# Cosine attention and a two-layer MLP in one kernel: three value and weight loads of GpSimd in another order

## The chip, the cores and the metric

One core of a Trainium2 chip. The metric is the device time of one execution in microseconds (us). The kernel before takes 432.26 us, the median of 3 runs (431.92 to 432.89).

## The reference

Eight batches, 12 heads, 448 positions, head size 64. Attention first, with queries and keys scaled to unit length:

```
q_n = q / (norm(q) + 1e-6);  k_n = k / (norm(k) + 1e-6)
scores = q_n @ k_n^T / tau
attn   = exp(scores - max) / (sum + 1e-9)
x      = (attn @ v), heads side by side          # 3584 x 768
h      = x @ w_in                                # 768 x 2048
out    = max(0.01 h, h) @ w_out                  # 2048 x 768
```

All inputs are float32, and so is the output.

## The kernel before

**Units of work.** A *pair* is two heads of one batch: 6 pairs to a batch, 48 in all, numbered by `s`. A *quad* is two pairs: 3 to a batch, 24 in all, numbered by `j`. The 448 positions of a sequence are 384 in three tiles of 128, and 64 left over; the leftovers of two pairs are packed together ("rem"). A *chunk* `c` is the 384 or 512 rows of the MLP that follow a batch.

**A pair's path.** `load_qk` (SP's queue) loads q and k in float32; the load pool has four buffers, so pair s+4 takes the place of pair s. `squares` (GpSimd) and `sums` (VectorE) give the sums of squares, `roots` (ScalarE) the norms, `normalise` (VectorE) the scaled bf16 tile `qn`. `transposes` turns it into `qkT` (TensorE up to pair 11, then by DMA). `scores` and `key_tiles` multiply on TensorE (L253), and ScalarE takes the exponential (L265). Ahead of each pair's squares `hold` has GpSimd cast one column of `qn` into a small tile, `seen`: it makes GpSimd wait there until VectorE has normalised a certain pair.

**A quad's path.** `attend(j)` runs `totals(j)` (products of the exponentials with ones, L276; then the reciprocal on ScalarE by Ln and Exp), two strips of `products(j, e)` with the values, also L276, and `scale(j, e)` on VectorE into `xT`. The products need two things from the values: `v_b`, the 384 main positions of that quad (`load_v(j)`, 192 KB, L143), and `v_rem`, the left-over 64 positions of a whole batch (`load_v_rem(b)`, four loads of 24 KB, L151; two tiles, by even and odd batch). In a strip the products with `v_b` come first (12 matmuls), then those with `v_rem` (4).

**The MLP.** `first(c, m)` is one of 16 groups of the first layer (L330), with a leaky ReLU on ScalarE (L337). `second(c, ts, half)` is 16 matmuls of the second layer (L360) for one half of the output's columns, which read that half of `w_out_sb`. For chunk 0 all of half 0 comes before half 1. The weights come by GpSimd's queue, cast from float32 to bf16: `load_w_in` in four parts of 768 KB (L106), `load_w_out(half)` in two of 1536 KB (L112).

**Order.** The schedule is written by hand; each engine runs its instructions in program order. First a loop over the six pairs of batch 0 (L468 to L523); its last slot, s == 5, is the one that is changed. Then a stretch written out (L536 to L574): `attend(2)`, and the preparation of pairs 7 to 10 between 13 of the 16 groups of chunk 0's first layer, with `load_v(4)` and `load_w_out(1)` in it. Then a planner's loop over batches 1 to 7: in each unit it places `attend`, three score tiles, the preparation of a pair ahead, and as many MLP groups as its share says. Its first unit for batch 1 begins with `attend(3)` and `load_v(5)`.

In the sixth slot GpSimd does, in order: `hold`, `squares(8)`, `load_w_out(0)`, `load_v(3)`, `load_v_rem(1)`. Quad 3 is the first of batch 1; `load_v(3)` and `load_v_rem(1)` are the values that `attend(3)` reads.

Of the kernel before, what the change touches and what calls it, by code (L numbers as in the profile page):

```python
# [16 lines left out]
def kernel(  # L17
# [59 lines left out]
    def banks(count, keep=None, which=None):  # L77
        lo, hi = (0, 8) if not deals["apart"] else (0, 4) if count == 2 else (4, 8)
        x = which if which is not None else min(
            (i for i in range(lo, hi, count) if not set(range(i, i + count)) & set(kept.values())),  # L80
            key=lambda i: max(age[i : i + count]),
        )
        deals["n"] += 1
        age[x : x + count] = [deals["n"]] * count
        if keep:
            kept[keep] = x
        return ps[:, x] if count == 1 else ps[:, x : x + count]
# [16 lines left out]
    def load_w_in(i):  # L104
        n0, e = i // 2 * (D_ff // 2), i % 2
        gp.dma_start(  # L106
            out=w_in_sb[:, e::2, n0 : n0 + D_ff // 2], in_=w_in_r[e, :, :, n0 : n0 + D_ff // 2]
        )

    def load_w_out(half):  # L110
        n0 = half * HALF
        gp.dma_start(out=w_out_sb[:, :, n0 : n0 + HALF], in_=w_out_r[:, :, n0 : n0 + HALF])  # L112
# [6 lines left out]
    def load_qk(s, engs=(nc.sync, nc.sync)):  # L119
        if s >= NSLOT:  # L120
            return
        b, h0 = s // NPAIR, 2 * (s % NPAIR)
        q_h = ldp.tile([128, 2, 4, D], F32, name="q_h")
        k_h = ldp.tile([128, 2, 3, D], F32, name="k_h")
        engs[0].dma_start(out=q_h[:, :, 0:3], in_=main(q, b, h0, 2))  # L125
        engs[1].dma_start(out=k_h, in_=main(k, b, h0, 2))
        for i, (x, eng) in enumerate(zip((q, k), engs)):
            eng.dma_start(  # L128
                out=q_h[64 * i : 64 * i + 64, :, 3],
                in_=x[b, h0 : h0 + 2, MAIN:S].rearrange("h p d -> p h d"),  # L130
            )
        raw[s] = (q_h, k_h)
# [5 lines left out]
    def load_v(j):  # L138
        if j >= B * NQ:
            return  # L140
        b, jj = divmod(j, NQ)
        vb[j] = vbp.tile([128, 4, 3, D], BF16, name="v_b")
        gp.dma_start(out=vb[j], in_=main(v, b, 4 * jj, 4))  # L143

    def load_v_rem(b):
        if b >= B:
            return
        r = v[b, :, MAIN:S].rearrange("(j g) p d -> g p j d", g=4)
        for g in range(4):
            lo = 64 * (g // 2)  # L150
            gp.dma_start(out=vrb[b % 2][lo : lo + 64, :, g], in_=r[g])  # L151
# [3 lines left out]
    def squares(s, engs=(gp, gp)):  # L155
        if s >= NSLOT:
            return
        tiles = []
        for x, eng, name in zip(raw[s], engs, ("sq0", "sq1")):
            sq = sqp.tile(list(x.shape), F32, name=name)  # L160
            if eng is nc.scalar:
                nc.scalar.activation(sq, x, func=AF.Square)
            else:
                eng.tensor_tensor(sq, x, x, op=ALU.mult)  # L164
            tiles.append(sq)
        sqs[s] = tiles

    def sums(s, parts=(0, 1)):
        if s >= NSLOT:
            return  # L170
        if s not in ss:
            ss[s] = smp.tile([128, 14], F32, name="ss")
        for i in parts:
            o = ss[s][:, 0:8] if i == 0 else ss[s][:, 8:14]
            nc.vector.tensor_reduce(  # L175
                o.rearrange("p (h t) -> p h t", h=2), sqs[s][i], axis=AX.X, op=ALU.add
            )

    def roots(s):
        if s >= NSLOT:  # L180
            return
        nc.scalar.activation(ss[s], ss[s], func=AF.Ln, bias=tiny)
        nc.scalar.activation(ss[s], ss[s], func=AF.Exp, scale=0.5)
        nc.scalar.activation(ss[s], ss[s], func=AF.Identity, bias=eps)  # L184
# [3 lines left out]
    def normalise(s):  # L188
        if s >= NSLOT:
            return  # L190
        r = smp.tile([128, 14], F32, name="r")
        nc.vector.reciprocal(r, ss[s])  # L192
        qn[s] = qnp.tile([128, 7, 2, D], BF16, name="qn")
        for x, lo, hi, r0 in ((raw[s][0], 0, 4, 0), (raw[s][1], 4, 7, 8)):
            nt = hi - lo
            nc.vector.tensor_tensor(  # L196
                qn[s][:, lo:hi],
                x.rearrange("p h t d -> p t h d"),
                r[:, r0 : r0 + 2 * nt].rearrange("p (h t) -> p t h", h=2)
                .unsqueeze(3).to_broadcast([128, nt, 2, D]),  # L200
                op=ALU.mult,
            )
# [19 lines left out]
    def transposes(s):  # L222
        if s >= NSLOT:
            return
        dst = qtp.tile([128, 7, 128], BF16, name="qkT")
        qkT[s] = dst.rearrange("p t c -> p (t c)")
        if s >= DMA_FROM:
            nc.sync.dma_start(
                out=dst, in_=qn[s].rearrange("p t h d -> p (t h d)"), transpose=True
            )  # L230
            return
        tp = transposed()
        one(tp, s, 0, 7)
        nc.vector.tensor_copy(out=dst, in_=tp)
# [3 lines left out]
    def scores(s, kis):  # L238
        key_tiles([(s, ki) for ki in kis])
# [53 lines left out]
    def products(j, e, po=None):  # L293
        b, jj = divmod(j, NQ)
        if po is None:
            po = banks(1, (j, e))
        pos[j, e] = po
        vm = vb[j].rearrange("p h t (d e) -> p h t e d", e=2)
        vr = vrb[b % 2].rearrange("p j g (d e) -> p j g e d", e=2)
        strip_products(j, po, lambda g, ki: vm[:, g, ki, e], lambda g: vr[:, jj, g, e])  # L300

    def scale(j, e):
        b, jj = divmod(j, NQ)
        m, half = divmod(b, 2)
        if m not in xT:
            xT[m] = xtp.tile([128, KT, 2 * S], BF16, name="xT")
        nc.vector.tensor_tensor(  # L307
            xT[m][:, 2 * jj + e, half * S : (half + 1) * S], pos.pop((j, e))[:, :S], rbs[j],
            op=ALU.mult,
        )  # L310
        if (j, e) in kept:
            given_back((j, e))
# [115 lines left out]
    def fill(count):  # L428
        wm = banks(1)
        for i in range(count):  # L430
            nc.tensor.matmul(
                out=wm, lhsT=warm[:, :128], rhs=warm, start=(i == 0), stop=(i == count - 1)
            )
# [4 lines left out]
    def hold(x):  # L438
        seen = smp.tile([128, 1], F32, name="seen")
        gp.tensor_copy(out=seen, in_=x)  # L440
# [27 lines left out]
    for s in range(NPAIR):  # L468
        j = s // 2 - 1 if s >= 2 else None
        even = s % 2 == 0  # L470
        n = s + 2 if s + 2 <= NPAIR else None
        if s != 3 and s != 5:
            scores(s, (0,))
        if s == 1:
            roots(2)
        if j is not None and not even:
            products(j, 1)
        scores(s, (1,))
        fill(2)
        if s and n:  # L480
            sums(n, (0,))
        normalise(s + 1)
        load_qk(s + 5)
        if j is not None and not even:
            scale(j, 0)
        hold(qn[s + 1][:, 6, 0, 0:1])
        squares(s + 3)
        if s == 5:
            load_w_out(0)
        if not even:  # L490
            load_v(s // 2 + 1)
        if s != 2 and s < 5:
            load_w_in(s - s // 3)
        if s == 5:
            load_v_rem(1)
        if n:
            sums(n, (1,))
        scores(s, (2,))
        if s == 5:

            scale(j, 1)
            for m in range(SOON):
                pms[0, m] = banks(1, (0, m, 0), 4 + m)
            first(0, 0, range(KT - 2))
        elif not even:
            fill(2)
        if not even:
            scores(s, (3,))
        transposes(s + 1)
        if s == 0:  # L510
            sums(2, (0,))
        if s == 5:
            first(0, 1, range(KT - 2))
        elif not even:
            fill(2)
        if n and s:
            roots(n)
        if j is not None and not even and s < 5:
            scale(j, 1)
        if j is not None and even:  # L520
            totals(j)
            scores(s + 1, (0,))
            products(j, 0)  # L523
# [11 lines left out]
    s, j = NPAIR, NQ - 1  # L535
# [61 lines left out]
    for b in range(1, B):  # L597
# [3 lines left out]
        for i, (at, tiles, ahead) in enumerate(units):  # L601
# [8 lines left out]
            s = b * NPAIR + ahead if ahead else NSLOT  # L610
# [63 lines left out]
```

## Time and profile before

| What | Value |
|---|---|
| Median of 3 runs | 432.26 us |
| Profiled execution, first to last instruction | 433.2 us |
| TensorE busy | 418.9 us, 97% |
| ScalarE busy | 267.7 us, 62% |
| VectorE busy | 188.4 us, 43% |
| GpSimd busy | 138.1 us, 32% |
| Mean granted TensorE clock | 0.995 |
| GpSimd's transfer queue | 25056 packets, 11.80 MB |
| SP's transfer queue | 77296 packets, 40.98 MB |

The profile is of a single execution; 433.2 us is its span, and of its own time no other figure is given. It is 0.96 us above the median of the timed runs. In the rows below, PE is TensorE, PEld its weight loads, DVE VectorE, ACT ScalarE, POOL GpSimd and SP SyncE; Lnnn is a line of the kernel before. "[1.18 <-DMA v_b...]" means that the engine sat idle for 1.18 us before the row and that a landing of `v_b` ended it.

### The profile page before, as it was taken

Reading aid. Unit: us, or ns where it says so; the run is one execution under the profiler, and the core shown is the slowest. Engines: PE = TensorE matmul, PEld = TensorE weight load, DVE = VectorE, ACT = ScalarE, POOL = GpSimd, SP = SyncE. Lnnn points to the kernel's source line nnn. Section 1 sums busy time; section 2 is a strip of 40 time slices with the busy share of each in tenths; the row PEclk is TensorE's granted clock in tenths of the full one; section 3 lists DMA queues with packets and bytes.
Section 4 is the critical chain, followed back from the end, with each engine's and each line's share of the span. In section 5 each row is a group of like instructions: output and inputs, shape, how many; then the busy total and the mean of one; then the engine's idle time right before and its main releaser. Section 6 shows DMA issues by size and latency. Waiting matters only on the chain.

```text
span 433.2 us, 8650 instructions
## 1 busy us (share of the span) xinstructions
PE 418.9 (97%) x3329; PEld 209.0 (48%) x3329; DVE 188.4 (43%) x366; ACT 267.7 (62%) x494; POOL 138.1 (32%) x208
## 2 busy tenths in 40 slices
PE   8699989999999999999999999999999999999995
PEld 3234535544455555544455555554455555554563
DVE  5875846643353544552444544643434432220021
ACT  4997846668654787658745687668845496434300
POOL 4767523261424133531334114432234120000000
PEclk9999989999999999999999999999999999999999
DMA  7999994795548447765448557666437532010022
GB/s 173 196 236 232 219 212 65 166 189 142 105 106 164 100 126 142 162 109 142 86 105 159 102 144 146 140 113 160 82 86 162 101 80 41 36 74 2 0 74 73
DMA packets 102889, 53.65 MB, mean 124 GB/s; under 512 B 68929, under 2 KB 97857, under 8 KB 102849
## 3 DMA queue, kind: packets, MB, share of 16 engines
q1 hardware_dynamic: 77296, 40.98, 37.9%
q0 software_dynamic: 25056, 11.80, 21.6%
q8 instruction: 26, 0.43, 0.4%
q10 hardware_dynamic: 496, 0.33, 0.2%
q14 instruction: 15, 0.11, 0.1%
HBM read 45.61 MB, written 11.01 MB: 131 GB/s over the span
## 4 chain that ended last, share of the span: by engine, by line
PE 85%; DMA 8%; POOL 3%; SPq 1%; DVE 1%; ACT 0%; issue 0%; POOLq 0%; DVEq 0%
PE ps L360 34%; PE ps L330 31%; PE ps L276 12%; PE ps L253 8%; DMA v_rem<-in_v_dram 5%; DMA q_h<-in_k_dram 3%; POOL sq L164 1%; DMA q_h<-in_q_dram 1%; SPq L128 1%; DVE qn L196 1%; POOL v_b L143 0%; POOL v_rem L151 0%; POOL w_out_sb L112 0%; PE ps L210 0%; SPq L125 0%
## 5 line engine op out<-in xcount | busy, mean ns | idle before, releaser
L265 ACT ACTIVATE pe<-ps 128x896 bf16<-128x896 f32 x144 | 122.5, 917 | 53.0 <-PE ps L253 52.0
L330 PE MATMUL ps<-xT,w_in_sb 128*128 128x384 bf16 (+1 forms) x768 | 151.4, 353 | 0.7 <-DVE xT L307 0.7
L360 PE MATMUL ps<-w_out_sb,hT 128*128 128x384 bf16 x896 | 151.9, 326 | 0.0
L360 PEld LDWEIGHTS <-hT 128*128 128x128 bf16 x896 | 85.2, 98 | 62.9 <-issue 8.0
L330 PEld LDWEIGHTS <-w_in_sb 128*128 128x128 bf16 x768 | 73.1, 98 | 73.1 <-issue 8.1
L337 ACT ACTIVATE hT<-ps 128x384 bf16<-128x384 f32 (+1 forms) x128 | 65.1, 540 | 40.1 <-PE ps L330 39.5
L440 POOL CAST seen<-qn 128x1 f32<-128x1 bf16 x47 | 8.7, 185 | 210.4 <-DVE qn L196 210.4
L371 DVE COPY osb<-ps 128x384 f32<-128x384 f32 (+1 forms) x56 | 30.9, 552 | 97.3 <-PE ps L360 90.9
L175 DVE TENSOR_REDUCE ss<-sq 128x8 f32<-128x512 f32 (+1 forms) x96 | 56.8, 613 | 18.5 <-POOL sq L164 16.5
L253 PE MATMUL ps<-qkT 64*128 64x448 bf16 (+1 forms) x384 | 46.7, 362 | 4.2 <-ACT pe L265 2.9
L164 POOL TENSOR_TENSOR sq<-q_h 128x512 f32<-128x512 f32 x46 | 47.8, 1039 | 5.0 <-DMA q_h<-in_k_dram 4.2
L192 DVE RECIPROCAL r<-ss 128x14 f32<-128x14 f32 x48 | 11.6, 241 | 82.3 <-ACT ss L184 82.3
L307 DVE TENSOR_TENSOR xT<-ps,rb 128x448 bf16<-128x448 f32 x48 | 27.9, 619 | 34.5 <-ACT rb L288 29.3
L164 POOL TENSOR_TENSOR sq<-k_h 128x384 f32<-128x384 f32 x46 | 38.7, 842 | 0.0
L276 PE MATMUL ps<-pe,v_b 128*32 128x448 bf16 x576 | 36.4, 357 | 1.2 <-DMA v_b<-in_v_dram 1.2
L287 ACT ACTIVATE rb<-ps 128x448 f32<-128x448 f32 x24 | 13.0, 543 | 35.7 <-PE ps L276 35.7
L196 DVE TENSOR_TENSOR qn<-q_h,r 128x512 bf16<-128x512 f32 x48 | 33.7, 702 | 1.9 <-DVE r L192 0.3
L253 PEld LDWEIGHTS <-qkT 64*128 64x128 bf16 (+1 forms) x384 | 13.0, 96 | 39.0 <-issue 32.7
L196 DVE TENSOR_TENSOR qn<-k_h,r 128x384 bf16<-128x384 f32 x48 | 27.7, 578 | 0.0
L265 ACT ACTIVATE pr<-ps 128x896 bf16<-128x896 f32 x24 | 22.2, 925 | 0.5 <-PE ps L253 0.5
L276 PEld LDWEIGHTS <-v_b 128*32 128x32 bf16 x576 | 15.2, 97 | 13.4 <-DMA v_b<-in_v_dram 1.6
L151 POOL DMA_DIRECT2D v_rem<-in_v_dram x32 | 20.4, 646 | 0.1
(39 smaller groups left out, 184.0 us busy)
## 6 DMA issues: line engine op xcount, KB each, us to landing
q_h<-in_q_dram SPq DMA_DIRECT2D x48, 192.0 KB, 3.1
k_h<-in_k_dram SPq DMA_DIRECT2D x47, 192.0 KB, 3.1
out_dram<-osb SPq DMA_DIRECT2D x30, 192.0 KB, 3.5
v_b<-in_v_dram POOLq DMA_DIRECT2D x24, 192.0 KB, 5.1
out_dram<-osb SPq DMA_DIRECT2D x12, 384.0 KB, 3.2
w_in_sb<-in_moe_w_in_dram POOLq DMA_DIRECT2D x4, 768.0 KB, 10.1
w_out_sb<-in_moe_w_out_dram POOLq DMA_DIRECT2D x2, 1536.0 KB, 18.2
q_h<-in_q_dram SPq DMA_DIRECT2D x48, 32.0 KB, 3.6
```

Source lines behind the costliest of these rows:

```text
L151: gp.dma_start(out=vrb[b % 2][lo : lo + 64, :, g], in_=r[g])
L164: eng.tensor_tensor(sq, x, x, op=ALU.mult)
L175: nc.vector.tensor_reduce(o.rearrange("p (h t) -> p h t", h=2), sqs[s][i], axis=AX.X, op=ALU.add)
L196: nc.vector.tensor_tensor(qn[s][:, lo:hi], x.rearrange("p h t d -> p t h d"), r[:, r0 : r0 + 2 * nt].rearrange("p (h t) -> p t h", h=2) .u ...
L253: nc.tensor.matmul(out=out[:, a, :S], lhsT=x[rows, c0:c1], rhs=x[rows, 0:S], start=True, stop=True,)
L265: nc.scalar.activation(out=dst, in_=sc[:, :, :S], func=AF.Exp, scale=inv_tau)
L276: nc.tensor.matmul(out=x[32 * g : 32 * g + 32, :S], lhsT=weights(g, ki) if ki < 3 else rem(g), rhs=pe[s][:, ki, a, :] if ki < 3 else pr[j] ...
L307: nc.vector.tensor_tensor(xT[m][:, 2 * jj + e, half * S : (half + 1) * S], pos.pop((j, e))[:, :S], rbs[j], op=ALU.mult,)
L330: nc.tensor.matmul(out=pm[:, :n], lhsT=w_in_sb[:, kt, m * 128 : (m + 1) * 128], rhs=xT[c // 2][:, kt, c0 : c0 + n], start=(kt == 0), stop= ...
L337: nc.scalar.activation(out=hT[c][:, m, :n], in_=pms.pop((c, m))[:, :n], func=AF.Prelu, alpha=0.01)
L360: nc.tensor.matmul(out=po2[:, :HALF], lhsT=hT[c][:, m, ts * 128 : (ts + 1) * 128], rhs=w_out_sb[:, m, half * HALF : (half + 1) * HALF], st ...
L371: nc.vector.tensor_copy(out=o[:, half * HALF : half * HALF + cut], in_=po2[:, :cut])
```

## The change

In the sixth slot `load_w_out(0)` is issued after `load_v(3)` and `load_v_rem(1)`, not before them.

```
         hold(qn[s + 1][:, 6, 0, 0:1])
         squares(s + 3)
-        if s == 5:
-            load_w_out(0)
         if not even:
             load_v(s // 2 + 1)
         if s != 2 and s < 5:
             load_w_in(s - s // 3)
         if s == 5:
             load_v_rem(1)
+            load_w_out(0)
         if n:
             sums(n, (1,))
```

The same instructions are issued with the same operands. Lines behind the change are numbered one lower in the changed kernel.

More of the change, by code (lines that the diff above doesn't have):

```diff
@@ L487 @@
         squares(s + 3)
-        if s == 5:
-            load_w_out(0)
         if not even:
@@ L495 @@
             load_v_rem(1)
+            load_w_out(0)
         if n:
```

## The prediction

> **What bounds the kernel now.** I read the page's busy shares and its chain first, then the chain in order of time, TensorE's timeline around the one place where that chain is not TensorE, the granted clock there, and last the transfers of GpSimd's queue.
>
> ```profile
> PE 418.9 (97%) x3329; PEld 209.0 (48%) x3329; DVE 188.4 (43%) x366; ACT 267.7 (62%) x494; POOL 138.1 (32%) x208
> ...
> PE 85%; DMA 8%; POOL 3%; SPq 1%; DVE 1%; ACT 0%; issue 0%; POOLq 0%; DVEq 0%
> ```
>
> TensorE is busy 97% of the span and holds 85% of the chain. A change pays only where TensorE is held up. The chain in order of time shows one such place near the change:
>
> ```profile
> 36.00 1.17 POOL w_out_sb L112
> 37.17 0.76 POOL v_b L143
> 37.92 1.22 POOL v_rem L151 x2
> 39.15 20.71 DMA v_rem<-in_v_dram
> 59.86 0.04 issue
> 59.91 2.23 PE ps L276 x18
> 62.14 1.24 PE ps L253 x6
> 63.37 0.74 PE ps L210 x7
> 64.11 2.92 PE ps L330 x18
> 67.04 0.67 PE ps L253 x6
> 67.71 2.71 PE ps L360 x16
> 70.42 0.39 PE ps L210 x7
> ...
> 76.91 2.38 PE ps L276 x48
> 79.29 0.67 PE ps L253 x6
> ```
>
> A piece is start, length, what. A 24 KB load of remaining values (v_rem, batch 1) is on the chain for 20.71 us, behind the issue of the 1536 KB half of w_out. From 59.91 to the last matmul there is nothing but TensorE. The 20.71 us are not the prize: TensorE worked through most of them. What it lost is in its timeline (start, busy, groups, idle before):
>
> ```profile
> 55.63 0.75 PE L276 MATMUL ps<-pe,ones 128*32 128x448 bf16 x12
> 56.20 0.36 PE L276 MATMUL ps<-pr,ones_rem 128*32 128x448 bf16 x4
> 57.75 0.75 PE L276 MATMUL ps<-pe,v_b 128*32 128x448 bf16 x12 [1.18 <-DMA v_b<-in_v_dram]
> 58.42 0.36 PE L276 MATMUL ps<-pr,v_rem 128*32 128x448 bf16 x1
> 59.07 0.36 PE L276 MATMUL ps<-pr,v_rem 128*32 128x448 bf16 x1 [0.28 <-DMA v_rem<-in_v_dram]
> ```
>
> This is attend(3), the first quad of batch 1. It starts at 55.63 and needs v_b(3) and v_rem(1); both come late. The granted clock after it (window, length, PE, PEld, DVE, ACT, POOL, clock, DMA share, GB/s):
>
> ```profile
> 60.00:61.00 1.00, 1.00 (x13) 0.46 (x16) 0.25 (x1) 0.00 (x0) 0.00 (x0) 0.72 1.32 202
> 61.00:62.00 1.00, 1.00 (x13) 0.15 (x1) 0.38 (x1) 0.00 (x0) 0.00 (x0) 0.50 1.32 206
> 62.00:63.00 1.00, 1.00 (x7) 0.29 (x6) 0.82 (x2) 0.31 (x1) 0.00 (x0) 0.50 1.32 206
> 63.00:64.00 1.00, 1.00 (x10) 0.70 (x9) 0.85 (x2) 1.00 (x2) 0.00 (x0) 0.57 1.30 203
> ```
>
> After the hole TensorE works some 3.5 us at about half clock; from 64 on the clock is 1.00 again.
>
> **The move on GpSimd.** The change moves one issue (w_out, 1.22 us by its row at 35.94) behind five (v_b 0.76 us, four of v_rem 2.49 us). Nothing is added. Put side by side, the instruction lists of the two kernels differ on GpSimd alone, in these six places. GpSimd ends the block at 40.40 either way and then idles 3.88 us until a cast at 44.28, so the reordering costs it nothing. Each of its DMA issues waits for the one eight places ahead in its list, as eight completion semaphores take turns. That of w_out is now the one of v_b(2), issued at 26.62 and landed 6.5 us later, at 33.1; it does not wait. v_b(5), issued at 58.01, used to wait for w_out's first half and now waits for v_b(3), which lands earlier. SP's queue is not touched.
>
> **The move in the transfer queue.** GpSimd's transfers land in the order of issue here. Issue start plus time to landing: last part of w_in 33.21 + 10.1 = 43.3; w_out first half 35.94 + 19.7 = 55.6; v_b(3) 37.16 + 20.5 = 57.7; last v_rem 39.15 + 20.71 = 59.9. So w_out had the queue for 12.3 us, v_b for 2.1, v_rem for 2.2. In the new order: v_b(3) at 43.3 + 2.1 = 45.4, v_rem at 47.6, w_out at 59.9. There is no gap at the head, since the w_in transfer covers the queue until 43.3 and w_out is issued by 40.4. The values are wanted at about 56.5 and 57.1: some 9 us of slack. A value load with nothing long ahead (v_b, median 5.1 us) would be down even earlier.
>
> **What TensorE wins.** With the values there, attend(3) takes what attend(4) takes, 2.38 us at full clock (row at 76.91), the six score matmuls 0.67 (79.29) and the seven transposes 0.39 (70.42): 3.44 us. Before, from the start of attend(3) to the first L330 matmul of the next group, it was 64.11 - 55.70 = 8.41 us (55.70 is the timeline's 55.63 put on the chain's clock, which runs 0.07 later throughout: 62.07 there is 62.14 here). The gain is 8.41 - 3.44 = 4.97 us. It has two parts. The clock: the second product strip 60.25 to 62.14 took 1.89 against 2.38/3 = 0.79, the scores 1.24 against 0.67, the transposes 0.74 against 0.39, together 2.02 us. The rest, 2.95 us, is waiting.
>
> **What is late next.** All that TensorE does after this comes 5 us earlier.
> - w_out's first half is first read by L360, at 67.71 - 4.97 = 62.74. I have it landing at 59.9: 2.8 us of slack where there were 12.1. Bounds: the other half (issued 52.27, landed 69.0, behind v_b(4) landed at 51.45 + 9.8 = 61.2) took 7.8 us in the queue with little else running, which would give 55.4; 12.3 us is its own row, among loads of q and k. I take 12.3, the same traffic. Cost nothing, and the overshoot beyond 62.74 one for one.
> - The loads of q and k of slots 10 to 13 share the DMA engines with this. Slot 10's last piece landed at 34.82 + 14.2 = 49.0, and GpSimd's squares waited 1.32 us for it. It now shares with 288 KB of values from 43.3 to 47.6, not with w_out. If it came later, the row sums at 52.38 have 0.9 us of room; then ACT's roots and TensorE would follow. I take 0, with +0.5 us as the end.
> - ACT: three exps 2.54 us, roots 0.9, two Prelus 0.85, one 0.49, begun about 58.4, end near 63.2, where TensorE is done with the group at 62.07. Before, TensorE's slow clock let ACT catch up. The banks that the scores and L360 want next are read out by about 62.5. Cost 0 to 0.3 us.
> - w_out's second half lands at 69.0 and is wanted at 79.97 - 5 = 75.0; v_b(4) at 61.2, wanted near 72.7. Covered.
>
> The clock part is the least sure term. The row is one execution: TensorE nearly idle from 56.6 to 59.9, clock down between 60 and 61. [...] I keep the row for the forecast and the case without it as a rival.
>
> **The sum.** Span 433.22 - 4.97 = 428.25. The span is 0.96 above the median of the timed runs, 432.26 (431.92 to 432.89); the same subtraction from the median gives 427.29. Costs of 0 to 0.3 for ACT and a share of the clock that may be missing in the median run: I say 427.4.
>
> **Rivals.**
> 1. *Only the wait is won.* If the timed runs of before mostly keep full clock after the hole, the gain is 2.95: 429.3. For it: the hole is short, and the profiled run is slower than the median by 0.96. Against: the fastest of three is only 0.34 below the median, not 2. Chance 0.10.
> 2. *Another wait takes over in part.* w_out lands 1 to 2.5 us after 62.74, or slot 10's load moves ACT's roots: gain 2.5 to 4, about 428.9. For it: slack only 2.8 us, estimated from one execution. Against: same bytes, same queue, the end of the block fixed at 59.9. Chance 0.10.
> 3. *Nothing moves*, because the transfers share the engines instead of following each other, and the values land at 57 to 60 still: 432.3. Against: v_b and v_rem landed 2 and 4 us after w_out, in steps, as a line does. Chance 0.03.
> 4. *Slower: the first L360 waits for w_out.* A wait of 2.95 us brings back the wait, and with the half clock after it all 4.97, so it turns at a landing of 65.7. A landing at 68.7, as w_out would have if it took 21 us in the queue, would be 6 + 2 - 5 = 3 us slower: 435.3. For it: it is the largest transfer and now last. Against: it would need 5.8 us more than its own row. Chance 0.03.
>
> The forecast itself has 0.74.
>
> **How the numbers follow.** About 0.2% (0.9 us) is what a measurement of this kernel can tell from no change. The forecast and rivals 1 and 2 are faster: 0.94. Rival 3 is the same, 0.03, rival 4 slower, 0.03. Range: the forecast spans 426.8 (full gain, with half a microsecond for a rerun of the kernel before) to 427.9; taking in most of rivals 1 and 2 brings it to 429.3, and leaves out 1 in 10.
>
> **What would show it.** Right: in the profile after, the chain has no v_rem load near 39 to 60; attend(3) starts at about 55.6 and takes 2.4 us; no clock below 1.00 between 56 and 68; the first L360 at about 62.7 without a wait for w_out_sb; the span near 428. Wrong step by step: a wait of TensorE on w_out_sb at 62.7 (queue estimate too short); waits of TensorE on ACT between 58 and 63; GpSimd waiting for q or k longer than 1.32 us at 49; attend(3) starting later than 55.6. The prediction fails if attend(3) is as long as before or if its gain is lost again before 77.

## The result, and the profile after

The changed kernel takes 430.30 us (median of 9 runs, 429.95 to 431.01), against 432.53 us for the kernel before (9 runs, 430.92 to 433.13). The ratio is 0.9951, with an interval of 0.9939 to 0.9962: faster by about 2.1 us by the ratio (the medians differ by 2.2), where 5 were forecast. The 430.30 lies outside the stated range.

And yet the profile after looks almost line for line as forecast. The page's first line, and its chain by engine:

```profile
span 428.1 us, 8636 instructions
...
PE 92%; DVE 3%; ACT 2%; DMA 1%; issue 1%; DVEq 0%; ACTq 0%
```

The forecast span was 428.25 us. The load of values has left the chain, and TensorE's share went from 85% to 92%. GpSimd's timeline of the block (start, length, group):

```profile
35.66 0.81 POOL L143 DMA_DIRECT2D v_b<-in_v_dram  x1
36.47 2.48 POOL L151 DMA_DIRECT2D v_rem<-in_v_dram  x4
38.94 1.21 POOL L112 DMA_DIRECT2D w_out_sb<-in_moe_w_out_dram  x1
44.00 0.18 POOL L440 CAST seen<-qn 128x1 f32<-128x1 bf16 x1 [3.85 <-DVE qn L196]
```

The issues take the same time in the new order, and GpSimd still idles behind them. Their landings, from the list of transfers issued between 36.7 and 39.2 us (size, us from issue to landing):

```profile
w_out_sb<-in_moe_w_out_dram POOLq DMA_DIRECT2D x1, 1536.0 KB, 17.7
v_rem<-in_v_dram POOLq DMA_DIRECT2D x4, 24.0 KB, 7.9
```

The remaining values land by about 46, ten us ahead of their use, and w_out at 38.94 + 17.7 = 56.6. TensorE's timeline at attend(3):

```profile
55.34 0.75 PE L276 MATMUL ps<-pe,ones 128*32 128x448 bf16 x12
55.92 0.36 PE L276 MATMUL ps<-pr,ones_rem 128*32 128x448 bf16 x4
56.11 0.74 PE L276 MATMUL ps<-pe,v_b 128*32 128x448 bf16 x12
...
57.73 0.74 PE L253 MATMUL ps<-qkT 64*128 64x448 bf16 x6
58.40 0.56 PE L210 MATMUL ps<-id,qn 128*128 128x128 bf16 x7
58.80 3.09 PE L330 MATMUL ps<-xT,w_in_sb 128*128 128x384 bf16 x18
61.83 0.74 PE L253 MATMUL ps<-qkT 64*128 64x448 bf16 x6
62.50 2.77 PE L360 MATMUL ps<-w_out_sb,hT 128*128 128x384 bf16 x16
```

No row has an idle time before it, and the granted clock is 1.00 from 54 to 67 us. attend(3) takes 57.73 - 55.34 = 2.39 us, and the first L360 starts at 62.50 without a wait. So the two profiles differ by 5.1 us (433.2 and 428.1), and the two medians by 2.2. In the changed kernel the profiled execution took 429.95 us, 1.85 more than its span. By that offset the profiled execution of before took some 435 us: longer than any of its nine timed runs. The open question is what a usual execution of the kernel before looks like.

### The profile page after: what moved, and what is told of

It reads as the page before. It is cut to its first block, busy times and chain, and to the rows that moved or that the text cites. A ratio compares the mean times of both kernels' runs of the same rounds, so it can differ in the third digit from the quotient of the medians.

```text
span 428.1 us, 8636 instructions
## 1 busy us (share of the span) xinstructions
PE 415.3 (97%) x3315; PEld 208.6 (49%) x3329; DVE 187.2 (44%) x366; ACT 267.6 (63%) x494; POOL 137.7 (32%) x208
## 4 chain that ended last, share of the span: by engine, by line
PE 92%; DVE 3%; ACT 2%; DMA 1%; issue 1%; DVEq 0%; ACTq 0%
PE ps L360 35%; PE ps L330 34%; PE ps L276 13%; PE ps L253 9%; PE ps L210 1%; DVE qn L196 1%; DMA q_h<-in_k_dram 1%; ACT pe L265 1%; DVE ss L175 1%; DVE xT L307 0%; DVE qkT L234 0%; ACT ss L184 0%; ACT ss L182 0%; DVE r L192 0%; PE ps L431 0%
## 5 line engine op out<-in xcount | busy, mean ns | idle before, releaser
L360 PE MATMUL ps<-w_out_sb,hT 128*128 128x384 bf16 x896 | 151.9, 326 | 0.0
L330 PE MATMUL ps<-xT,w_in_sb 128*128 128x384 bf16 (+1 forms) x757 | 150.6, 352 | 1.1 <-DVE xT L307 0.5
L360 PEld LDWEIGHTS <-hT 128*128 128x128 bf16 x896 | 85.2, 98 | 62.9 <-issue 8.4
L330 PEld LDWEIGHTS <-w_in_sb 128*128 128x128 bf16 x768 | 73.1, 98 | 73.0 <-issue 7.9
```

The costliest lines, as they stand in the source:

```text
L330: nc.tensor.matmul(out=pm[:, :n], lhsT=w_in_sb[:, kt, m * 128 : (m + 1) * 128], rhs=xT[c // 2][:, kt, c0 : c0 + n], start=(kt == 0), stop= ...
L360: nc.tensor.matmul(out=po2[:, :HALF], lhsT=hT[c][:, m, ts * 128 : (ts + 1) * 128], rhs=w_out_sb[:, m, half * HALF : (half + 1) * HALF], st ...
```

## The experiments

Three theories. A: the profiled execution of before is typical. B: the wait at attend(3) is typical, the half clock after it is not. C: the values mostly land earlier than they did in that execution.

**The kernel before, again.** No edit.

> The kernel before, unchanged, to see how its executions differ. In the changed kernel an execution's time is 1.85 us above its span (429.95 for 428.1); by that the profiled span of 433.2 belongs to a time near 435.1, which none of nine timed runs (430.92 to 433.13) has. Theory A (the profiled execution is typical): spans near 433 us and clock near 0.995 in most runs. Theory B (half clock after the hole is rare): spans near 431, 2.0 us under the profiled one, the wait of TensorE at attend(3) still about 2.95 us, granted clock 1.00 between 60 and 64 us. Theory C (the values mostly land earlier than in the profiled execution): spans near 431, and in the profile the last v_rem lands clearly before 59.9 us, the wait being shorter than 2.95 us.

433.35 us (12 runs, 432.49 to 435.33), against 433.09 in the runs of before beside it: 1.0004 (0.9981 to 1.0027). The profiled execution took 433.08 us with a span of 431.2, which is usual. Its attend(3):

```profile
56.19 0.75 PE L276 MATMUL ps<-pe,ones 128*32 128x448 bf16 x12
56.77 0.36 PE L276 MATMUL ps<-pr,ones_rem 128*32 128x448 bf16 x4
57.27 0.75 PE L276 MATMUL ps<-pe,v_b 128*32 128x448 bf16 x12
57.85 0.36 PE L276 MATMUL ps<-pr,v_rem 128*32 128x448 bf16 x1
58.56 0.36 PE L276 MATMUL ps<-pr,v_rem 128*32 128x448 bf16 x1 [0.36 <-DMA v_rem<-in_v_dram]
59.27 0.36 PE L276 MATMUL ps<-pr,v_rem 128*32 128x448 bf16 x1 [0.34 <-DMA v_rem<-in_v_dram]
59.81 0.36 PE L276 MATMUL ps<-pr,v_rem 128*32 128x448 bf16 x1 [0.18 <-DMA v_rem<-in_v_dram]
...
60.86 0.74 PE L253 MATMUL ps<-qkT 64*128 64x448 bf16 x6
```

and the granted clock (window, length, busy times of PE, PEld, DVE, ACT and POOL, clock, DMA share, GB/s):

```profile
58.00:60.00 2.00, 1.12 (x11) 0.31 (x10) 0.00 (x0) 0.33 (x1) 1.21 (x2) 1.00 1.31 213
60.00:62.00 2.00, 2.00 (x31) 0.99 (x24) 1.66 (x3) 0.71 (x1) 0.00 (x0) 1.00 1.33 202
62.00:64.00 2.00, 2.00 (x15) 1.21 (x13) 1.17 (x3) 2.00 (x4) 0.00 (x0) 1.00 1.31 204
```

The hole is there, the half clock behind it is not: 1.00 from 54 to 68 us. This execution does have a stretch at half clock, but long before, where the first profile has 1.00:

```profile
12.00:16.00 4.00, 2.80 (x15) 0.75 (x14) 3.35 (x6) 3.20 (x6) 3.28 (x5) 0.74 0.98 216
16.00:20.00 4.00, 3.71 (x24) 1.09 (x23) 3.07 (x7) 3.90 (x9) 1.86 (x3) 0.84 0.97 167
```

The last of the four v_rem loads is on the chain here, issued at 40.32 and down 19.45 us later; TensorE goes on at 59.81. In the first profile the chain runs through the third of them. The fourth came later, as TensorE's weight loads show:

```profile
60.24 0.09 PEld L276 LDWEIGHTS <-v_rem 128*32 128x32 bf16 x1 [0.24 <-DMA v_rem<-in_v_dram]
```

attend(3) took 4.67 us here, 2.28 over its full-speed time of 2.39. At full clock the scores follow the last landing by 1.05 us (59.81 to 60.86). By that count the first profile would have come to them at 61.29 without its slow clock, a loss of 3.27 us. Here the loss is 0.99 us smaller: 0.56 because TensorE began attend(3) later (56.19, not 55.63), and 0.43 because the last landing was earlier. A falls, B is right about the clock behind the hole, and C has some part in the smaller wait.

**Two more profiles of before**, each of a single execution. No edit.

> The kernel before, a further profile with the time of the same execution. Theory B: a time of 432.5 to 433.7 goes with a wait of 2 to 2.5 us at attend(3) and a clock of 1.00 between 60 and 64; a time near 435 goes with 0.50 there. Theory C (landings vary): the time follows the landing of v_rem, with 1.00 in all of them.

> The same once more. Theory B: as for the look before; by the spread of the timed runs one in five or six would show the half clock after the hole. Theory C: the time follows the landing of v_rem.

The first took 433.77 us, span 431.9; the second 432.87, span 431.0. The start of attend(3), its first late row and the next scores, in the first:

```profile
54.88 0.75 PE L276 MATMUL ps<-pe,ones 128*32 128x448 bf16 x12
...
58.30 0.76 PE L276 MATMUL ps<-pe,v_b 128*32 128x448 bf16 x12 [2.49 <-DMA v_b<-in_v_dram]
...
61.54 0.74 PE L253 MATMUL ps<-qkT 64*128 64x448 bf16 x6
```

and its clock:

```profile
56.00:58.00 2.00, 0.00 (x0) 0.00 (x0) 0.00 (x0) 0.99 (x2) 2.00 (x3) 1.00 1.43 228
58.00:60.00 2.00, 1.27 (x14) 0.42 (x14) 0.00 (x0) 0.00 (x0) 0.33 (x1) 1.00 1.49 191
60.00:61.00 1.00, 1.00 (x14) 0.43 (x17) 0.04 (x1) 0.00 (x0) 0.00 (x0) 1.00 1.35 202
```

TensorE was there early, stood still for 2 us and more, lost 4.27 us at attend(3), and kept the full clock. In the second attend(3) ran from 56.02 to 60.65, a loss of 2.24 us, again at 1.00 from 54 to 68 us. So neither has the half clock behind the hole (the second has it between 13.8 and 17.3 us). Their times differ by 0.9 us, and so do their ends of attend(3), 61.54 and 60.65, and the moments at which the last v_rem let TensorE go on, 60.48 and 59.60. The time follows the landing here, as C says, while the losses (4.27 and 2.24) differ by 2.0 us.

These profiles fit one line: the span is the start of the scores after attend(3) plus 370.3 to 370.4 us (60.86 + 370.3 = 431.2; 61.54 + 370.4 = 431.9; 60.65 + 370.35 = 431.0; after: 57.73 + 370.4 = 428.1). The first profile of before has more, 62.07 + 371.1, since there the half clock reaches into the scores and transposes.

**A longer hole.**

```
         if s == 5:
             load_w_out(0)
+            spare = cpool.tile([128, 4, 3, D], BF16, name="spare")
+            gp.dma_start(out=spare, in_=main(v, 1, 0, 4))
         if not even:
             load_v(s // 2 + 1)
```

> The kernel before with one more load of 192 KB into a spare tile, issued between w_out's first half and load_v(3); nothing reads the tile. The values land some 2 us later, so the hole at attend(3) grows from 2.3 us to about 4.3 us. Theory B: the longer hole brings on the half clock in most executions, so it costs the 2 us of delay and 1 to 2 us of clock: 3 to 4 us slower than before in the median, with 0.50 in the rows of the granted clock after the hole. Rival (the half clock has nothing to do with this hole): 2 us slower, clock 1.00 after it.

435.0 us against 432.74 beside it: 1.0046 (1.0029 to 1.0063), 2.0 us slower. The six runs form two groups, 433.61 and 433.84, and 434.96 to 435.76. The profiled one took 435.26 us, span 433.1:

```profile
58.83 0.75 PE L276 MATMUL ps<-pe,v_b 128*32 128x448 bf16 x12 [2.16 <-DMA v_b<-in_v_dram]
...
62.36 1.18 PE L253 MATMUL ps<-qkT 64*128 64x448 bf16 x6
```

```profile
60.00:61.00 1.00, 1.00 (x10) 0.61 (x14) 0.00 (x0) 0.00 (x0) 0.00 (x0) 0.50 1.34 203
61.00:62.00 1.00, 1.00 (x14) 0.56 (x6) 0.62 (x1) 0.00 (x0) 0.00 (x0) 0.50 1.33 207
62.00:63.00 1.00, 1.00 (x9) 0.29 (x6) 0.53 (x1) 0.01 (x1) 0.00 (x0) 0.50 1.31 204
```

Here are both in one execution: a time of 435 and a clock of 0.50 after the hole. Three to 4 us were expected. The load itself costs about 1 us, not 2 (433.7 in the lower group against 432.74): the last v_rem let TensorE go on at 60.23, within the 59.60 to 60.48 of the profiles of before, so what grew, against three of those four, is the standstill ahead of v_b (2.16 us). The gap between the groups, some 1.5 us, is about what the half clock is worth (1.6 us in the first profile of before, worked out below). Four of six runs were in the upper group, and none of the 13 runs of before on this chip took over 434 us.

Of 69 runs of the kernel before, over all the chips used, 9 took more than 434 us, all on one chip. The mean clocks, on record for 60 of the 69, fit a half clock in these: 0.990 to 0.995 in all nine, while none of the 34 runs with 0.997 or more took over 433.8. But a mean does not say where the clock was low, and 17 shorter runs have 0.993 to 0.996. Nor is it the only way to such a time: with only `load_v(3)` ahead, the profiled execution took 434.24 us with 1.00 after the hole and a late landing, and a run with filler 434.23 with a mean clock of 1.000 (both below). Which of the nine had the half clock there is not shown.

The stretches at half clock are about equally long: 0.50 from 60.44 to 63.85, 3.41 us, in the first profile of before (0.72 over the first microsecond and 0.57 over the last, in the prediction's rows), and by the rows about 59.9 to 63.3 with the longer hole (0.97 over 58 to 60, 0.85 over 63 to 64) and 13.9 to 17.3 in the repeat of before (0.74 and 0.84). Where they lie in the kernel differs from execution to execution. The same hole drew the half clock in the first profile of before, with a standstill of 1.18 us ahead of v_b, and not in three others, one of which stood still there for 2.49 us. What decides between the two is not shown.

**Filler in the hole.**

```
         totals(j)
+        if j == NQ:
+            was = age[:], deals["n"]
+            fill(4)
+            age[:], deals["n"] = was
         po = banks(2)
```

> The kernel before, with four extra matmuls of 128x512 on constants (0.22 us each, results unused) on TensorE between the totals and the products of attend(3). They lie in the hole and take 0.86 us of it; the waits for the values are not touched. Theory A (half clock follows the hole in most executions): the filler shortens the idle stretch, full clock stays, the kernel is up to 2.0 us faster. Theory B (half clock is rare): no change within 0.3 us. Theory C (values mostly there early): slower by 0 to 0.9 us, since the filler then delays the products.

433.13 us against 433.09: 0.9995 (0.9978 to 1.0012), no change. Twelve runs between 432.09 and 434.23. In its profile the scores start at 60.41 and the clock is 1.00 from 54 to 68 us. This is what theory B expects: in most executions there was no half clock for the filler to prevent. That none of the twelve is above 434.3 fits, but twelve runs are too few to call it shown.

**One half of the move at a time.** Only `load_v(3)` ahead of w_out:

```
-        if s == 5:
-            load_w_out(0)
         if not even:
             load_v(s // 2 + 1)
+        if s == 5:
+            load_w_out(0)
```

> Only load_v(3) is issued ahead of w_out's first half; load_v_rem(1) stays behind. The products with v_b then start at once and TensorE waits for v_rem alone. By the profiled execution v_rem lands last of all in either order, at about 59.9 us, so attend(3) still ends late: the wait is 0.57 us of matmuls less at most. Theory A and B: gain 0.5 to 1 us of the 2.1, the rest stays. Theory C (landings vary): the gain may be anything from 0 to 1 us. If it gained all 2.1 us, the wait for v_b would be the cause and not that for v_rem.

432.63 us (431.98 to 435.46) against 433.09: 0.9998 (0.9978 to 1.0019). The products with v_b start at once, and TensorE waits one step later, until 60.97 for the last v_rem:

```profile
57.09 0.74 PE L276 MATMUL ps<-pe,v_b 128*32 128x448 bf16 x12
59.00 0.36 PE L276 MATMUL ps<-pr,v_rem 128*32 128x448 bf16 x1 [1.18 <-DMA v_rem<-in_v_dram]
```

Only `load_v_rem(1)` ahead:

```
         if s == 5:
+            load_v_rem(1)
             load_w_out(0)
         if not even:
             load_v(s // 2 + 1)
...
-        if s == 5:
-            load_v_rem(1)
```

> Only load_v_rem(1) is issued ahead of w_out's first half; load_v(3) stays behind it and now lands last in the block, near 59.9 us by the profiled execution of before. The products wait for v_b at 56.5 us until then, 3.4 us, and then run without further waits. Theories A and B: about as long as before, up to 0.5 us slower. Theory C: v_b lands 1 to 2 us earlier than 59.9, time as before or up to 1 us faster. In no theory does it gain the full 2.1 us.

432.44 us (431.94 to 437.54) against 433.09: 0.9993 (0.9964 to 1.0022). Now v_b ends the wait, and lands at 58.5:

```profile
58.51 0.75 PE L276 MATMUL ps<-pe,v_b 128*32 128x448 bf16 x12 [1.40 <-DMA v_b<-in_v_dram]
59.08 0.36 PE L276 MATMUL ps<-pr,v_rem 128*32 128x448 bf16 x4
```

Neither half can be told from no change: whichever load stays behind w_out lands between 58.5 and 61 in these two profiles, and attend(3) cannot end before. The gain belongs to the two together.

**The changed kernel again**, on the chip of the longer hole and of the two further profiles.

> The changed kernel again, on the chip and beside the runs of the kernels below. Theory B (the wait at attend(3), about 2.3 us in a typical execution, is all that is won, and the half clock is a matter of some executions of before): 2.0 to 2.6 us faster in the median, ratio near 0.995, and no execution of it near 435 us. Theory A (5 us, half clock included): ratio near 0.9885.

430.63 us (430.30 to 430.72) against 432.74: 0.9952 (0.9940 to 0.9964), the same 2.1 us. Its attend(3) runs from 55.69 to 58.07, its span is 428.4. Over both sets 14 runs lie between 429.95 and 431.01; before has a spread of 5 us over all chips, and of 2.2 us on this one. Without the hole TensorE waits for no landing, and the clock is 1.00 from 54 to 67 us in both profiles of this kernel. The early half clock is still there in the first of this kernel's two profiles (14.78 to 18.19 us), and the time does not follow it: that execution, with a mean clock of 0.996, took 429.95 us, and the runs with 1.000 took 430.10 to 431.01.

## Why the prediction was wrong, and where it was right

**Right, step by step.** The three loads landed in the order of their issue in both kernels: w_out at 55.6, v_b(3) at 57.7 and the last v_rem by 60.24 before, v_b(3) at 44.4, v_rem by about 46 and w_out at 56.6 after. GpSimd lost nothing. attend(3) at full speed takes 2.39 us (2.38 said), and from its start to the next L330 it is 3.46 (3.44 said). The first L360 comes at 62.50 (62.74 said, less 0.07 for the two clocks of the views) and waits for nothing. w_out landed at 56.6 and not 59.9, so it had more room than said. ACT cost nothing, and GpSimd's wait of 1.32 us for pair 10's load was gone: the squares at 47.64 have none. Neither rival 2 nor rival 4 occurred; rival 3 falls with the landings of the values.

**Wrong: the gain of 4.97 us, taken off the median.** Both its terms were read from one execution, and together they were too large for a usual one.
- *The clock, 2.02 us.* It is 0 in three of four profiled executions of before (1.00 from 60 to 64 us). This is rival 1, which had a chance of 0.10. Even in the first profile the half clock cost some 1.6 us: 0.78 up to the scores (62.07 for 61.29) and 0.80 from there to L330 (1.88 for 1.08). The prediction priced the second strip at 0.79, where right behind a landing it takes 1.05 at full clock (59.81 to 60.86, and 59.60 to 60.65), and took the strip's start (60.25) and end (62.14) from two views that lie 0.07 us apart.
- *The wait, 2.95 us.* It was read as if TensorE always came to attend(3) at 55.6 and the values always landed as late; by the count above it was 3.27 in that execution, with a last landing at 60.24 (the prediction's 59.9 is that of the third v_rem). TensorE came between 54.88 and 56.19 in the four profiles of before. There this hardly counts, since the end hangs on the landing; in the changed kernel it counts in full (55.34 and 55.69, spans of 428.1 and 428.4). What makes TensorE come earlier or later is open. In the executions whose time is nearest to their median (433.08 and 432.87) the loss is 2.28 and 2.24 us, and 432.53 less 2.26 is 430.3, as measured. Rival 1 kept the 2.95, and so gave 429.3. That the figures meet so closely is luck: the first of the two further profiles lost 4.27 us, with a time 1 us above its median, and the execution of 430.30 on the same chip is 0.3 us below its own.

**The step that failed is the sum:** "the same subtraction from the median gives 427.29". The prediction saw a span 0.96 us above the median and took it for a shift that both kernels share. But a span belongs below the time of its execution here: in the nine profiled executions that have both, the time is 1.84 to 2.16 us longer. A span 0.96 above the median thus said that the profiled execution was some 2.8 us longer than usual (0.96 + 1.85), and 2.8 us is what the gain was overstated by (4.97 - 2.2). The argument against rival 1 ("the fastest of three is only 0.34 below the median, not 2") looked on the wrong side: by their times (431.92 to 432.89) the three timed runs had the full clock behind the hole, though no clock is on record for them, and the profile was the one without. Only the later runs gave the offset of 1.85; with it, the forecast span of 428.25 gives 430.1 for the changed kernel, within 0.2 us of what was measured: its own end was forecast well, its starting point was not the median.

## What to carry to other kernels

Before a loss read from a profile is taken off a median, put the profiled execution's time beside the timed ones; if its span is already as long as they are (433.2 against 432.26, where the times were some 1.85 above the spans), part of the loss is its own. Where a wait ends at a landing, its length says little: TensorE came at 54.88 in one profile and at 56.02 in another and lost 4.27 and 2.24 us, but was done only 0.9 us apart, so count from the end of the wait, not from its length. Where a queue lands its loads in order, as here, put the small loads that are wanted soon ahead of the large one that is wanted late, and all of them: with one left behind the time was 432.63 and 432.44 us against 433.09, no change, and with none 430.30 against 432.53.

## What the runs showed of the hardware

The half clock after a hole was not a matter of the hole's length alone: TensorE at a standstill of 2.49 us, up to 58.30, kept 1.00 in one execution, and a hole with single matmuls in it, after a standstill of 1.18 us, went to 0.50 at 60.44 in another. And a 24 KB load took 20.7 us behind a 1536 KB one in the same queue, 7.9 us when it was issued ahead of it, behind the last part of w_in and v_b(3).

The clock also dropped far from the hole: 6 of the 10 profiles have one stretch of about 3.4 us at 0.50 between 13.7 and 18.2 us, early in the kernel (0.50 from 14.78 to 18.19 in the changed kernel). None of these has another after the hole, and the two that have one there (the first profile of before and the longer hole) have none early. That does not mean that one excludes the other: by estimate one stretch takes 0.004 off the mean clock (half of 3.41 us in 431), and means of 0.990 and, with only `load_v_rem(1)` ahead, 0.987 (the run of 437.54 us) point to two or more in one execution. No profile shows two in its rows (8 to 24 and 54 to 67 us).
